# A gated state-space mix on one core: v's loads last and integer angles in the head, a room of its own for the ninth pair, three row products later, one group of output matmuls a scan later

## The chip, the core and the metric

The kernel runs on one core of one Trainium2 chip. Its time is the device time of one execution in microseconds; the measure is the median of several runs. One core has these engines, each with its own instruction stream: TensorE (PE) for matrix products, VectorE (DVE), ScalarE (ACT, which also evaluates functions from tables), GpSimd (POOL) and SyncE (SP). In this kernel SP starts nearly all loads and stores, and POOL starts the accumulating transfers: a transfer that adds what it reads to what stands in its target, called a gather below.

## What is computed

Two sequence layers over the same x (2048 steps, 1024 channels, bf16), mixed by a gate for each step:

```python
g = sigmoid((x * gate_w).sum(-1, keepdims=True))

# layer A: diagonal complex state space with 1024 states
Lam_bar = exp(dt * Lam)
Bu = einsum("bld,pd->blp", x, ((Lam_bar - 1) / Lam)[:, None] * Bmat)
for t in range(L):
    h = Lam_bar * h + Bu[:, t]
y_a = 2 * einsum("blp,dp->bld", hseq, Cmat).real + x * Dskip

# layer B: shift convolution of k (4 taps), times v, long convolution with ssm_k
kv = k_shift * v
y_b = x * (irfft(rfft(kv, 2S) * rfft(ssm_k, 2S))[:S] + kv * ssm_D)

out = g * y_a + (1 - g) * y_b
```

## The kernel before, in words

**Order.** Nothing is left to a scheduler on the four compute engines and SP. Every instruction goes through `put` (lines 92 to 95), which chains it behind the last one of the same engine; so every row of the profile has line 94, and groups are told apart by tiles. What the Python code calls first runs first on its engine. Most stages are generators: `step(x)` issues the next part of stage x, `steps(x, n)` the next n, `run(x)` the rest. `gather` (126) starts an accumulating transfer from POOL, `move` and `load_t` (a transposing load) start one from SP. Pools of tiles decide the rest: an instruction that writes a tile waits until the readers of the tile that had the room before are done. The pool `wu`, reached by `u4` (83), has three buffers of about 4 KB a partition, and `ps2` (86) hands out PSUM in four pieces of two banks.

**Layer B** goes over 8 tiles of 128 channels. `taps` (571) multiplies shifted columns of kT, the transposed k, by diagonal matrices `dg` on PE, and `times_v` multiplies by v on DVE. `fold_columns` or `fold_K` split the long filter into even and odd parts ("eok"), and `times_v` the same for the signal with its mirror image. `fwd_K` (634) and `fwd_V` (672) are forward transforms as matmuls with cosine and sine tables CF, SF and NCF (= -CF), in four steps `fi`; ACT evicts each result to KH (in BT[2], BT[3]) or Vh. `products` (685) multiplies the spectra on DVE, with gathers for some of the sums. `inverse` (767) transforms back with the tables CI and SI; ACT evicts to `cv`, and the result goes to a DRAM scratch, to be read back later by rows.

**The head** is channel tile 0, written out by hand (lines 157 to 174). Its loads on SP: two halves of kT, kn (the filter); v's first half is on ACT's queue, ahead of everything there but the small parameters, and v's second half on SP behind kn. DVE makes the angles of CF and SF in float32: the angle index over 4096 (`hf`), rounding with a large constant, the difference `rq` (`reduced`, 281), a Sin on ACT for SF, the absolute value on DVE, a Sin for CF. `first_times_v` (586) multiplies the tap sums by v straight from PSUM, forms the mirror image and its sum and difference. `first_K` (650) does the first two steps of the filter's transform, and evicts one on ACT and one on DVE. `inverse_angles` and `inverse_table` (382 to 398) make SI and CI from integer angles: an AND with 2047, an Abs on ACT (`fa`) and two Sin. `state_params` (418, "sp") computes from A's parameters the decay, the angles and the coefficients of all 8 tiles of states, in tiles of 128 x 8 or 16; its first part is an Exp on ACT (`dtv`), another table set than Sin. `taps(1)` starts the second channel tile, and its product with v on DVE (`ks<-ks,v`) is the start of a chain of DVE work.

**Layer A** goes over 4 blocks of 512 steps (tb) and 4 pairs of state tiles (g), 16 pairs in all. `Bu(i)` (833) multiplies x with B on PE for pair i of the list `order` (816), and ACT evicts to a tile U (odd and even steps apart). `turn_U` (922) scales the odd half by lambda on ACT to tiles Q and lets two gathers add it to the even half. U 6, 7, 8 and 15 come from the shared pool `wu`. `scan(tb, g)` (941) does the recurrence on DVE: turning by tables, four scan instructions, turning back; then it scales the states by lambda (`scaled`), on DVE, or for scans 4, 12, 13 and 14 on ACT into Q tiles, in which case the call is kept in `put_off` and made later. `sums` adds them to U's odd half during the next scan. `turn_C` turns the columns of C in the same way.

**Output rows.** 16 rows of 128 steps. For row k: `loads` reads layer B's result (pbb) and x (xr); `scale_b` (1076) scales pbb and Dskip's row on ACT, and a gather adds the two; `product` (1107) multiplies by x on DVE; `Cy_g` (1087) multiplies the states with C on PE; `scale_a` (1101) evicts from PSUM on ACT with the gate; `combine` (1111) starts a gather that adds the two; `store` writes the row out.

**The plan** (1433 to 1534) sets what stands between the scans. After scan j (`advance`), `plan[j]` names the PE work: "B9" is pair 9 of `Bu`, "C0" a whole output row, and "G23" is pair g = 3 of block 2 for all four rows of the block (`Cy_group`, 1471). With g = 3 the rows are done: for each of the four, `scale_a` and `combine` follow, and ahead of the first in block 2 the scaling that `put_off` holds. `multiplied[j]` names the row products that stand inside scan j, `scaled_b[j]` the rows whose `scale_b` comes after it; for a "G" entry they come ahead of the group. If `put_off` still holds a scaling when the plan entry is done, it is issued there. After the last scan the rows of block 3 follow: lines 1549 to 1567.

Of the kernel before, what the change touches and what calls it, by code (L numbers as in the profile page):

```python
# [15 lines left out]
MAGIC = 12582912.0  # L16
# [4 lines left out]
def kernel(  # L21
# [143 lines left out]
    for i, ap in enumerate((A_log_dt, A_Lambda_re, A_Lambda_im)):  # L165
        nc.scalar.dma_start(out=prow[i * ND:(i + 1) * ND, :], in_=ap.rearrange("(j p) -> j p", p=128))
    nc.scalar.dma_start(out=v0_half(0)[0], in_=v0_half(0)[1])
    pih = consts.tile([128, 1], F32, name="pih")
    put("dve", nc.vector.memset, pih, math.pi / 2.0)
    magic = consts.tile([128, 1], F32, name="magic")  # L170
    put("dve", nc.vector.memset, magic, MAGIC)

# [62 lines left out]
    for h in range(2):  # L235
        hs = slice(h * S // 2, (h + 1) * S // 2)
        load_t(kT0[:, PAD + hs.start:PAD + hs.stop], kf[hs, 0:128])
    load("kn", 0)
    move(*v0_half(1))
    lds["kT", 0], lds["v", 0] = kT0, v0  # L240
# [39 lines left out]

    def reduced(h, n):
        rq = u4([128, n], F32, "rq")
        ts(rq, h, MAGIC, -MAGIC, ALU.add, ALU.add)
        tt(rq, h, rq, ALU.subtract)
        return rq

    CF = tab_pool.tile([128, 2, 512], BF16, name="CF")
# [14 lines left out]


    stamp = consts.tile([128, 2], BF16, name="stamp")
    refl = consts.tile([128, 2, 128], BF16, name="refl")
# [8 lines left out]
    colm = consts.tile([128, 2], F32, name="colm")  # L314
    ts(colm, colm_i, 1.0 / 4096.0, None, ALU.mult)
    fr_ = u4([128, 512], F32, "fr_")
    copy(fr_, fr_i)
    pcol = consts.tile([128, 3 + KS, ND], F32, name="pcol")
# [5 lines left out]
    for k in range(KS):  # L324
        mm(psp[:, 1, k * ND:(k + 1) * ND], skr[:, :, k], ident[32:32 + ND, 32:32 + ND], True, True)
    hf = u4([128, 2, 512], F32, "h")
    for mt in range(2):
        ts(hf[:, mt], fr_, colm[:, mt:mt + 1], None, ALU.mult)
    copy(pcol[:, 3:], psp[:, 1, 0:KS * ND].rearrange("p (i j) -> p i j", j=ND))
# [37 lines left out]

    rqf = reduced(flat(hf), 1024)

    inv = {}  # L370

    def inverse_cols():
        colf = iota_i32([128, 2], [[512, 2]], 1, 4, "colf")
        inv["col"] = consts.tile([128, 2], F32, name="colneg")
        inv["at0"] = consts.tile([128, 2], F32, name="colat0")
        act(inv["col"], colf, func=ACT.Copy, scale=-1.0)
        act(inv["at0"], colf, func=ACT.Copy, scale=511.0)
        inv["less"] = consts.tile([128, 3], F32, name="less")
        for k, v in enumerate((-1024.0, -math.pi, -math.pi / 2.0)):
            nc.gpsimd.memset(inv["less"][:, k:k + 1], v)  # L380

# [8 lines left out]
    def inverse_table():  # L390

        hi, less, unit = flat(inv["room"]), inv["less"], TWO_PI / 2048.0
        fa = u4([128, 1024], F32, "fa")
        act(fa, hi, func=ACT.Abs, bias=less[:, 0:1])
        yield
        act(flat(SI), hi, func=ACT.Sin, scale=unit, bias=less[:, 1:2])
        yield
        act(flat(CI), fa, func=ACT.Sin, scale=unit, bias=less[:, 2:3])

# [18 lines left out]
    def state_params():  # L418

        dtv = small("dtv")  # L420
        act(dtv, logdt, func=ACT.Exp)
        yield
        abv = pair("abv")
        tt(abv, bc(dtv[:, None], [128, 2, NP]), pcol[:, 1:3], ALU.mult)
        yield
        act(rv, abv[:, 0], func=ACT.Exp)
        ts(thn, abv[:, 1], 1.0 / TWO_PI, None, ALU.mult)
        ts(nthn, abv[:, 1], -1.0 / TWO_PI, None, ALU.mult)
        yield
        th = pair("th")  # L430
        copy(th[:, 0], thn)
        ts(th[:, 1], thn, float(TB), None, ALU.mult)
        sq = pair("sq")
        tt(sq, pcol[:, 1:3], pcol[:, 1:3], ALU.mult)
        fr = pair("fr")
        ts(fr, th, MAGIC, -MAGIC, ALU.add, ALU.add)
        invden = small("invden")
        tt(invden, sq[:, 0], sq[:, 1], ALU.add)
        tt(fr, th, fr, ALU.subtract)
        put("dve", V.reciprocal, invden, invden)  # L440
        yield
# [208 lines left out]
    def first_K():  # L650

        eo, KH[0] = eos["k", 0], spectrum("K", 0)
        pss = [ps2([128, 2, 4, 128], "psk") for fi in range(2)]
        for mt in range(2):
            for fi, ps in enumerate(pss):
                fsl = slice(fi * 128, (fi + 1) * 128)
                for cc in range(2):
                    mm(ps[:, cc], (CF, SF)[cc][:, mt, fsl], eo[:, cc, mt], mt == 0, False)
                    mm(ps[:, cc, 1:4], (SF, NCF)[cc][:, mt, fsl], eo[:, 1 - cc, mt, 0:3], False, mt == 1)
                if mt == 1 and fi == 0:  # L660
                    act(of_tile(KH[0], fi), ps, func=ACT.Copy)
                elif mt == 1:
                    copy(of_tile(KH[0], fi), ps)

# [20 lines left out]
    def products(c, h=0, home=u4, by_dma=True):  # L685
# [147 lines left out]
    def Bu(i):  # L833
# [307 lines left out]
    step(columns)  # L1141
    sp = state_params()
    step(sp)
    step(first)
    ts(NCF, CF, -1.0, None, ALU.mult)
# [207 lines left out]
    load_CT(3)  # L1353
    with tc.tile_pool(name="fin", bufs=1, side="right") as fin:

        count = iter(range(16))

        def room(shape, dt, name):
            return fin.tile(shape, dt, name=name, tag=f"fin{next(count)}")

        prod, back = products(c, 0, room, False), inverse(c - 1)
        run(old)
        steps(prod, 3)
        run(turns_U[3])
        run(next(tiles))
        steps(turning[0], 2)
        step(back)
        run(back)
        gate(1)
        gate(2)  # L1370
        steps(prod, 2)
        b6, b7 = Bu(6)
        run(b6)
        run(b7)
        run(turns_U[6])
        run(turning[0])
        run(prod)
        load_xT(3)
        b8, b9 = Bu(7)
        run(b8)  # L1380
        run(b9)
        run(turning[1])
        b10, b11 = Bu(8)
        run(b10)
        run(b11)
    back = inverse(c)
# [37 lines left out]
    def Cy(tb, tl):  # L1424
        ps = ps2([128, 2, 512], "psy")
        for g in range(NG):
# [59 lines left out]
    for j in range(NS):  # L1486
# [109 lines left out]
```

## Time and profile before

| what | value |
|---|---|
| median of 3 runs | 379.9 us |
| the three runs | 379.87, 379.90, 380.58 us |
| time of the profiled execution | 381.04 us |
| its span, first to last instruction | 379.3 us |
| granted TensorE clock, mean | 1.00 |
| idle of ACT in the span | 71.7 us (379.3 - 307.6) |
| data moved by DMA | 71.78 MB, 189 GB/s |

Of the page's chain of work that ended last, this line tells whose work it was by engine:

```profile
DVE 55%; PE 26%; issue 8%; DMA 5%; ACT 4%; POOL 0%; SPq 0%; POOLq 0%; DVEq 0%
```

How to read the rows: a busy row of the page gives for each engine the busy time, its share of the span, and the number of instructions. A timeline row begins with the start in us from the span's beginning and the duration, then engine, line, operation, output <- inputs with their shapes, and how many equal instructions in a row it stands for (their first start, their whole length). What stands in brackets is the time for which the engine was idle just before, and what released it. PE is the matmul itself, PEld its weight load beside it. An engine that is idle in a row with no one waiting for it costs nothing.

### The profile page before, as it was taken

To read this page: it belongs to the slowest core of one execution; us is meant where nothing else is said; L and a number is where in the kernel's file an instruction comes from. 1 tells how busy PE (TensorE), PEld (TensorE's weight loads), DVE (VectorE), ACT (ScalarE), POOL (GpSimd) and SP (SyncE) were. 2 spreads that over 40 slices of the span, in tenths; PEclk is the share of its full clock that TensorE was granted. 3 is DMA by queue.
4 is the path that set the end of the run, shared out by engine and by line. 5 is a ranking of instruction groups with operands and counts; after the bars stand their busy time and mean duration, and the time that the engine had idled before them with its cause. 6 is when DMAs were issued, how large, how long until landed. Compare 5 with 4: busy or idle time off the path is not lost.

```text
span 379.3 us, 6647 instructions
## 1 busy us (share of the span) xinstructions
PE 369.9 (98%) x2434; PEld 200.3 (53%) x2469; DVE 364.1 (96%) x585; ACT 307.6 (81%) x473; POOL 79.1 (21%) x109
## 2 busy tenths in 40 slices
PE   7999999999999999999999999989999999999996
PEld 4656467575674847644544444434445444444444
DVE  8899999999999999999999999999999989969984
ACT  5879998988979899697949799998879868938501
POOL 4011030110301102021002012123443313635000
PEclk9999999999999999999999999999999999999999
DMA  7889999999999989968999999947998999998902
GB/s 168 168 114 264 215 213 189 236 218 203 228 200 185 215 166 194 179 145 153 207 183 209 215 186 253 256 101 131 197 247 138 251 247 204 160 255 146 221 0 111
DMA packets 126259, 71.78 MB, mean 189 GB/s; under 512 B 104649, under 2 KB 107601, under 8 KB 126226
## 3 DMA queue, kind: packets, MB, share of 16 engines
q1 hardware_dynamic: 112416, 45.90, 56.1%
q0 software_dynamic: 12688, 25.17, 38.7%
q10 hardware_dynamic: 1122, 0.28, 0.4%
q8 instruction: 19, 0.31, 0.3%
q14 instruction: 14, 0.11, 0.1%
HBM read 15.48 MB, written 8.39 MB: 63 GB/s over the span
## 4 chain that ended last, share of the span: by engine, by line
DVE 55%; PE 26%; issue 8%; DMA 5%; ACT 4%; POOL 0%; SPq 0%; POOLq 0%; DVEq 0%
PE psy L94 23%; DVE acc L94 20%; DVE wkh L94 13%; DVE A L94 5%; DVE Vh L94 4%; DVE t L94 3%; DVE U L94 2%; DVE ks L94 2%; DMA U<-Q 2%; ACT Q L94 2%; DVE trn L94 2%; PE taps L94 1%; DMA kT<-in_B_k_dram 1%; DMA BT<-gd 1%; DVE CT L94 1%
## 5 line engine op out<-in xcount | busy, mean ns | idle before, releaser
L94 PE MATMUL psy<-CT,U 128*128 128x512 bf16 (+1 forms) x418 | 92.7, 374 | 0.4
L94 PEld LDWEIGHTS <-U 128*128 128x128 bf16 x492 | 48.0, 98 | 57.3 <-issue 2.1
L94 PEld LDWEIGHTS <-BT 128*128 128x128 bf16 x544 | 50.5, 98 | 33.5 <-issue 0.2
L94 DVE TENSOR_TENSOR wkh<-BT,Vh 128x2048 bf16<-128x2048 bf16 (+3 forms) x31 | 44.6, 1457 | 0.0
L94 ACT ACTIVATE Q<-U,lam 128x512 bf16<-128x512 bf16 (+1 forms) x64 | 37.5, 632 | 8.5 <-DVE U L94 8.5
L94 POOL DMA_DIRECT2D U<-Q x26 | 26.6, 1033 | 82.9 <-ACT Q L94 42.4
L94 DVE TENSOR_TENSOR acc<-BT,Vh 128x4096 bf16<-128x4096 bf16 (+3 forms) x19 | 36.9, 1947 | 0.3 <-ACT Vh L94 0.2
L94 PE MATMUL both<-xT,BT 128*128 128x512 bf16 x157 | 35.2, 379 | 0.2
L94 ACT ACTIVATE Vh<-psv 128x1024 bf16<-128x1024 f32 x32 | 30.7, 1034 | 5.7 <-PE psv L94 5.6
L94 DVE TENSOR_TENSOR_SCAN A<-rv,init,A 128x256 bf16<-128x256 f32 x48 | 34.4, 738 | 0.0
L94 DVE TENSOR_TENSOR acc<-acc,wkh 128x1024 bf16<-128x1024 bf16 (+4 forms) x30 | 32.7, 1128 | 0.1
L94 ACT ACTIVATE U<-both 128x512 bf16<-128x512 f32 x44 | 24.2, 594 | 10.4 <-PE both L94 10.1
L94 ACT ACTIVATE BT<-psk 128x1024 bf16<-128x1024 f32 x31 | 30.0, 1035 | 2.3 <-PE psk L94 2.2
L94 POOL DMA_DIRECT2D acc<-wkh x8 | 9.7, 1218 | 100.7 <-DVE wkh L94 100.7
L94 PE MATMUL psk<-eok,SF 128*128 128x384 bf16 (+1 forms) x118 | 28.0, 354 | 0.2
L94 PEld LDWEIGHTS <-SF 128*128 128x128 bf16 x184 | 18.0, 98 | 19.1 <-issue 0.4
L94 PE MATMUL psz<-Vh,CI 128*128 128x512 bf16 x64 | 24.3, 379 | 0.0
L94 PE MATMUL psz<-Vh,SI 128*128 128x512 bf16 x64 | 24.3, 379 | 0.0
L94 PE MATMUL taps<-dg,kT 128*128 128x128 bf16 (+1 forms) x352 | 21.5, 208 | 1.0 <-DMA kT<-in_B_k_dram 1.0
L94 PEld LDWEIGHTS <-kT 128*128 128x128 bf16 x352 | 20.8, 99 | 2.5 <-DMA kT<-in_B_k_dram 2.0
L94 DVE TENSOR_TENSOR U<-U,trn 128x512 bf16<-128x512 bf16 (+1 forms) x58 | 21.2, 391 | 0.1
L94 PE MATMUL both<-xT,BTl 128*128 128x512 bf16 x94 | 21.1, 379 | 0.1
(223 smaller groups left out, 767.5 us busy)
## 6 DMA issues: line engine op xcount, KB each, us to landing
U<-Q POOLq DMA_DIRECT2D x26, 256.0 KB, 5.4
acc<-wkh POOLq DMA_DIRECT2D x6, 768.0 KB, 8.7
cv_scr<-cv SPq DMA_DIRECT2D x16, 256.0 KB, 4.8
kn<-in_B_ssm_k_dram SPq DMA_DIRECT2D x5, 512.0 KB, 3.7
v<-in_B_v_dram SPq DMA_DIRECT2D x5, 512.0 KB, 5.9
out_dram<-m SPq DMA_DIRECT2D x8, 256.0 KB, 4.8
BT<-cv_scr SPq DMA_DIRECT2D x7, 256.0 KB, 7.0
out_dram<-BT SPq DMA_DIRECT2D x7, 256.0 KB, 2.0
```

Of the source, the lines that this page charges most:

```text
L94: i = f(*a, **kw)
```

## The change

There are four parts.

- *Head.* v's first half leaves ACT's queue and goes on SP's, behind both halves of kT and kn. The angles of CF and SF become integers (minus the step times the odd index, then an AND with 4095), so `reduced` goes; the absolute value is an Abs on ACT to a tile `away`, and the Sin take scale and offset from `less`. The order is new: the first ACT part of `inverse_angles` comes right after CF and the second behind the folds, the parts of `state_params` later, NCF ahead of the products with v, `first_K` between the second of these and the mirror image. The second eviction of `first_K` goes from DVE to ACT. In `products(0, 0)` the first three pieces are in another order. Some parameter operations are placed in other parts of `state_params`.
- *A room.* The pool `fin`, which held one tile of channel tile 7's `products` for a limited stretch, stays open (in the diff only the lines that change more than their indentation), its tiles share one buffer, and U 8 (the ninth pair) is taken from it in place of `wu`.
- *Products.* Products 4, 7 and 11 leave scans 8, 10 and 12, and are issued after `advance` of these.
- *Group.* G23 moves from plan entry 12 to entry 13, ahead of which `scale_b` of row 15 stands; and so the put-off scaling of scan 12, which was issued inside G23, is issued at the end of entry 12, and the one issued inside G23 is that of scan 13.

```diff
@@ -166,7 +166,4 @@
         nc.scalar.dma_start(out=prow[i * ND:(i + 1) * ND, :], in_=ap.rearrange("(j p) -> j p", p=128))
-    nc.scalar.dma_start(out=v0_half(0)[0], in_=v0_half(0)[1])
     pih = consts.tile([128, 1], F32, name="pih")
     put("dve", nc.vector.memset, pih, math.pi / 2.0)
-    magic = consts.tile([128, 1], F32, name="magic")
-    put("dve", nc.vector.memset, magic, MAGIC)
 
@@ -238,2 +235,3 @@
     load("kn", 0)
+    move(*v0_half(0))
     move(*v0_half(1))
@@ -280,8 +278,2 @@
 
-    def reduced(h, n):
-        rq = u4([128, n], F32, "rq")
-        ts(rq, h, MAGIC, -MAGIC, ALU.add, ALU.add)
-        tt(rq, h, rq, ALU.subtract)
-        return rq
-
     CF = tab_pool.tile([128, 2, 512], BF16, name="CF")
@@ -303,2 +295,5 @@
 
+    less = consts.tile([128, 4], F32, name="less")
+    for k, v in enumerate((-2048.0, -1024.0, -math.pi, -math.pi / 2.0)):
+        nc.gpsimd.memset(less[:, k:k + 1], v)
     stamp = consts.tile([128, 2], BF16, name="stamp")
@@ -314,5 +309,3 @@
     colm = consts.tile([128, 2], F32, name="colm")
-    ts(colm, colm_i, 1.0 / 4096.0, None, ALU.mult)
-    fr_ = u4([128, 512], F32, "fr_")
-    copy(fr_, fr_i)
+    ts(colm, colm_i, -1.0, None, ALU.mult)
     pcol = consts.tile([128, 3 + KS, ND], F32, name="pcol")
@@ -325,5 +318,5 @@
         mm(psp[:, 1, k * ND:(k + 1) * ND], skr[:, :, k], ident[32:32 + ND, 32:32 + ND], True, True)
-    hf = u4([128, 2, 512], F32, "h")
+    hf = u4([128, 2, 512], I32, "h")
     for mt in range(2):
-        ts(hf[:, mt], fr_, colm[:, mt:mt + 1], None, ALU.mult)
+        ts(hf[:, mt], fr_i, colm[:, mt:mt + 1], None, ALU.mult)
     copy(pcol[:, 3:], psp[:, 1, 0:KS * ND].rearrange("p (i j) -> p i j", j=ND))
@@ -367,3 +360,3 @@
 
-    rqf = reduced(flat(hf), 1024)
+    ts(flat(hf), flat(hf), 4095, None, ALU.bitwise_and)
 
@@ -377,5 +370,2 @@
         act(inv["at0"], colf, func=ACT.Copy, scale=511.0)
-        inv["less"] = consts.tile([128, 3], F32, name="less")
-        for k, v in enumerate((-1024.0, -math.pi, -math.pi / 2.0)):
-            nc.gpsimd.memset(inv["less"][:, k:k + 1], v)
 
@@ -391,9 +381,9 @@
 
-        hi, less, unit = flat(inv["room"]), inv["less"], TWO_PI / 2048.0
+        hi, unit = flat(inv["room"]), TWO_PI / 2048.0
         fa = u4([128, 1024], F32, "fa")
-        act(fa, hi, func=ACT.Abs, bias=less[:, 0:1])
+        act(fa, hi, func=ACT.Abs, bias=less[:, 1:2])
         yield
-        act(flat(SI), hi, func=ACT.Sin, scale=unit, bias=less[:, 1:2])
+        act(flat(SI), hi, func=ACT.Sin, scale=unit, bias=less[:, 2:3])
         yield
-        act(flat(CI), fa, func=ACT.Sin, scale=unit, bias=less[:, 2:3])
+        act(flat(CI), fa, func=ACT.Sin, scale=unit, bias=less[:, 3:4])
 
@@ -419,2 +409,8 @@
 
+        sq = pair("sq")
+        tt(sq, pcol[:, 1:3], pcol[:, 1:3], ALU.mult)
+        invden = small("invden")
+        tt(invden, sq[:, 0], sq[:, 1], ALU.add)
+        put("dve", V.reciprocal, invden, invden)
+        yield
         dtv = small("dtv")
@@ -424,18 +420,11 @@
         tt(abv, bc(dtv[:, None], [128, 2, NP]), pcol[:, 1:3], ALU.mult)
-        yield
         act(rv, abv[:, 0], func=ACT.Exp)
-        ts(thn, abv[:, 1], 1.0 / TWO_PI, None, ALU.mult)
-        ts(nthn, abv[:, 1], -1.0 / TWO_PI, None, ALU.mult)
         yield
-        th = pair("th")
-        copy(th[:, 0], thn)
-        ts(th[:, 1], thn, float(TB), None, ALU.mult)
-        sq = pair("sq")
-        tt(sq, pcol[:, 1:3], pcol[:, 1:3], ALU.mult)
-        fr = pair("fr")
+        th, fr = pair("th"), pair("fr")
+        ts(th[:, 0], abv[:, 1], 1.0 / TWO_PI, None, ALU.mult)
+        ts(th[:, 1], abv[:, 1], TB / TWO_PI, None, ALU.mult)
+        copy(thn, th[:, 0])
         ts(fr, th, MAGIC, -MAGIC, ALU.add, ALU.add)
-        invden = small("invden")
-        tt(invden, sq[:, 0], sq[:, 1], ALU.add)
+        ts(nthn, thn, -1.0, None, ALU.mult)
         tt(fr, th, fr, ALU.subtract)
-        put("dve", V.reciprocal, invden, invden)
         yield
@@ -659,6 +648,6 @@
                     mm(ps[:, cc, 1:4], (SF, NCF)[cc][:, mt, fsl], eo[:, 1 - cc, mt, 0:3], False, mt == 1)
-                if mt == 1 and fi == 0:
+                if mt == 1:
                     act(of_tile(KH[0], fi), ps, func=ACT.Copy)
-                elif mt == 1:
-                    copy(of_tile(KH[0], fi), ps)
+                elif fi == 0:
+                    yield
 
@@ -702,6 +691,8 @@
 
-        def first(k):
+        split = c == 0 and h == 0
+
+        def first(k, fs=(0, 1)):
 
-            for f in range(2 if c == 0 and h == 0 else 1):
-                x = slice(f * 128, f * 128 + 128) if c == 0 and h == 0 else slice(0, w)
+            for f in fs if split else (0,):
+                x = slice(f * 128, f * 128 + 128) if split else slice(0, w)
                 tt(A[:, k, :, :, x], bc(K[:, k:k + 1, 0:1, x], [128, 2, 4, x.stop - x.start]), Vt[:, :, :, x], ALU.mult)
@@ -712,3 +703,8 @@
         if by_dma:
-            first(0)
+            if split:
+                first(0, (0,))
+                first(1, (0,))
+                first(0, (1,))
+            else:
+                first(0)
             yield
@@ -717,3 +713,3 @@
             yield
-            first(1)
+            first(1, (1,))
             yield
@@ -846,3 +842,5 @@
             shape = [128, 2 * (4 * HB + 4)]
-            if i in (6, 7, 8, 15):
+            if i == 8:
+                U = s5p["last"](shape, BF16, "U")
+            elif i in (6, 7, 15):
                 U = u4(shape, BF16, "U")
@@ -1130,2 +1128,3 @@
     step(first)
+    unit = TWO_PI / 4096.0
     trow[0] = tab_pool.tile([128, TB], mybir.dt.float16, name="row")
@@ -1133,9 +1132,10 @@
     inverse_cols()
-    act(flat(SF), rqf, func=ACT.Sin, scale=TWO_PI)
-    put("dve", V.scalar_tensor_tensor, out=flat(hf), in0=rqf, scalar=-1.0, in1=rqf, op0=ALU.mult, op1=ALU.max)
-    act(flat(CF), flat(hf), func=ACT.Sin, bias=pih, scale=-TWO_PI)
+    act(flat(SF), flat(hf), func=ACT.Sin, scale=unit, bias=less[:, 2:3])
+    away = u4([128, 1024], F32, "away")
+    act(away, flat(hf), func=ACT.Abs, bias=less[:, 0:1])
+    act(flat(CF), away, func=ACT.Sin, scale=unit, bias=less[:, 3:4])
+    angles = inverse_angles()
+    turns = inverse_table()
+    step(angles)
     columns = columns()
-    step(first)
-    fk = fold_columns(0)
-    step(fk)
     step(columns)
@@ -1143,12 +1143,13 @@
     step(sp)
-    step(first)
+    fk = fold_columns(0)
+    step(fk)
     ts(NCF, CF, -1.0, None, ALU.mult)
-    step(sp)
+    step(first)
+    step(first)
     run(fk)
-    angles = inverse_angles()
-    turns = inverse_table()
     step(angles)
-    step(angles)
-    step(sp)
+    fK = first_K()
+    step(fK)
     run(first)
+    run(fK)
     dg1 = dgs(1, True)
@@ -1157,5 +1158,5 @@
     load("kn", 1)
-    first_K()
     run(angles)
     fwd_V(0, (0, 1))
+    step(sp)
     step(turns)
@@ -1164,3 +1165,5 @@
     p0 = products(0, 0)
-    steps(p0, 3)
+    step(p0)
+    step(sp)
+    steps(p0, 2)
     run(columns)
@@ -1353,34 +1356,34 @@
     load_CT(3)
-    with tc.tile_pool(name="fin", bufs=1, side="right") as fin:
+    fin = pool("fin", 1, side="right")
 
-        count = iter(range(16))
+    def room(shape, dt, name):
+        return fin.tile(shape, dt, name=name, tag="fin")
 
-        def room(shape, dt, name):
-            return fin.tile(shape, dt, name=name, tag=f"fin{next(count)}")
+    s5p["last"] = room
 
...
@@ -1433,7 +1436,8 @@
     NS = NTB * NG
-    plan = ["", "B9 B10", "B11", "B12 B13 C0", "C1", "C2", "C3 B14", "B15", "G10", "G11", "G12 G13", "G20", "G21 G22 G23",
-            "", "", ""]
+    plan = ["", "B9 B10", "B11", "B12 B13 C0", "C1", "C2", "C3 B14", "B15", "G10", "G11", "G12 G13", "G20", "G21 G22",
+            "G23", "", ""]
     turned = dict(zip(range(3, 12), (8, 9, 4, 10, 11, 12, 13, 14, 15)))
     turned[0] = 7
-    multiplied = {4: (1,), 5: (2,), 6: (3,), 8: (4,), 9: (5,), 10: (6, 7), 11: (8,), 12: (9, 10)}
+    multiplied = {4: (1,), 5: (2,), 6: (3,), 9: (5,), 10: (6,), 11: (8,), 12: (9, 10)}
+    behind = {8: 4, 10: 7, 12: 11}
     loaded = {7: (7, 8), 8: (9, 10), 9: (11, 12), 10: (13,), 11: (14,), 12: (15,)}
@@ -1449,4 +1453,2 @@
             run(turning[6])
-        if j == 12:
-            product(11)
 
@@ -1493,2 +1495,4 @@
         advance(j)
+        if j in behind:
+            product(behind[j])
         for t in turning[2 * j:2 * j + 2]:
```

More of the change, by code (lines that the diff above doesn't have):

```diff
@@ L424, in state_params @@
         tt(abv, bc(dtv[:, None], [128, 2, NP]), pcol[:, 1:3], ALU.mult)
+        act(rv, abv[:, 0], func=ACT.Exp)
         yield
-        act(rv, abv[:, 0], func=ACT.Exp)
-        ts(thn, abv[:, 1], 1.0 / TWO_PI, None, ALU.mult)
-        ts(nthn, abv[:, 1], -1.0 / TWO_PI, None, ALU.mult)
-        yield
-        th = pair("th")
-        copy(th[:, 0], thn)
-        ts(th[:, 1], thn, float(TB), None, ALU.mult)
-        sq = pair("sq")
-        tt(sq, pcol[:, 1:3], pcol[:, 1:3], ALU.mult)
-        fr = pair("fr")
+        th, fr = pair("th"), pair("fr")
+        ts(th[:, 0], abv[:, 1], 1.0 / TWO_PI, None, ALU.mult)
+        ts(th[:, 1], abv[:, 1], TB / TWO_PI, None, ALU.mult)
+        copy(thn, th[:, 0])
         ts(fr, th, MAGIC, -MAGIC, ALU.add, ALU.add)
-        invden = small("invden")
-        tt(invden, sq[:, 0], sq[:, 1], ALU.add)
+        ts(nthn, thn, -1.0, None, ALU.mult)
         tt(fr, th, fr, ALU.subtract)
-        put("dve", V.reciprocal, invden, invden)
         yield
@@ L1143 @@
     step(sp)
+    fk = fold_columns(0)
+    step(fk)
+    ts(NCF, CF, -1.0, None, ALU.mult)
     step(first)
-    ts(NCF, CF, -1.0, None, ALU.mult)
-    step(sp)
+    step(first)
     run(fk)
-    angles = inverse_angles()
-    turns = inverse_table()
     step(angles)
-    step(angles)
-    step(sp)
+    fK = first_K()
+    step(fK)
     run(first)
+    run(fK)
     dg1 = dgs(1, True)
@@ L1353 @@
     load_CT(3)
-    with tc.tile_pool(name="fin", bufs=1, side="right") as fin:
-        count = iter(range(16))
-        def room(shape, dt, name):
-            return fin.tile(shape, dt, name=name, tag=f"fin{next(count)}")
[L1361 to L1385, printed above, removed]
+    fin = pool("fin", 1, side="right")
+    def room(shape, dt, name):
+        return fin.tile(shape, dt, name=name, tag="fin")
+    s5p["last"] = room
+    prod, back = products(c, 0, room, False), inverse(c - 1)
+    run(old)
+    steps(prod, 3)
+    run(turns_U[3])
+    run(next(tiles))
+    steps(turning[0], 2)
+    step(back)
+    run(back)
+    gate(1)
+    gate(2)
+    steps(prod, 2)
+    b6, b7 = Bu(6)
+    run(b6)
+    run(b7)
+    run(turns_U[6])
+    run(turning[0])
+    run(prod)
+    load_xT(3)
+    b8, b9 = Bu(7)
+    run(b8)
+    run(b9)
+    run(turning[1])
+    b10, b11 = Bu(8)
+    run(b10)
+    run(b11)
     back = inverse(c)
```

## The prediction

> **What bounds the kernel now.** I read the page's busy times first, then the windows, the chain in order of time, and the timelines of the three places that the change touches. From the page and from the windows (columns: stretch, its length, busy time and count of PE, PEld, DVE, ACT, POOL, granted clock, DMA share, GB/s):
>
> ```profile
> PE 369.9 (98%) x2434; PEld 200.3 (53%) x2469; DVE 364.1 (96%) x585; ACT 307.6 (81%) x473; POOL 79.1 (21%) x109
> ```
>
> ```profile
> 230.00:240.00 10.00, 9.95 (x47) 4.51 (x46) 10.00 (x23) 9.90 (x16) 3.73 (x5) 1.00 1.20 236
> 240.00:250.00 10.00, 8.76 (x40) 3.92 (x40) 9.90 (x25) 9.94 (x15) 1.83 (x3) 1.00 0.94 217
> 340.00:360.00 20.00, 19.95 (x93) 9.10 (x93) 20.00 (x42) 13.87 (x18) 6.10 (x7) 1.00 0.92 188
> ```
>
> A full stretch holds 47 matmuls of 512 columns in 10 us, 0.21 us each, at a granted clock of 1.00. PE is packed; the stretch from 240 has 40. So time is won only where PE stands still, and lost wherever PE comes to stand. The chain (start, length, engine):
>
> ```profile
> 22.02 1.09 DVE ks L94
> ...
> 43.48 1.22 DVE Vh L94
> ```
>
> PE has two stalls of note of its own, 0.97 us in the head at 7.48 and 1.51 us at 250.32 (rows below; in brackets stands the idle time before a row and what ended it). In between the chain runs through DVE, which from 22 us has no wait worth naming until 289; PE takes Vh at 43.6 as soon as DVE has half of it. So what the head does to DVE at 22 us is what it is worth.
>
> **Part 1, the head** (v's loads, integer angles, the new order).
>
> ```profile
> 4.34 2.17 PE L94 MATMUL taps<-dg,kT 128*128 128x128 bf16 x32
> 4.16 1.10 DVE L94 TENSOR_SCALAR rq<-h 128x1024 f32<-128x1024 f32 x1
> 5.29 1.23 DVE L94 TENSOR_TENSOR rq<-h,rq 128x1024 f32<-128x1024 f32 x1
> 6.55 1.06 ACT L94 ACTIVATE SF<-rq 128x1024 bf16<-128x1024 f32 x1 [0.65 <-DVE rq L94]
> 7.48 1.96 PE L94 MATMUL taps<-dg,kT 128*128 128x128 bf16 x32 [0.97 <-DMA kT<-in_B_k_dram]
> 7.81 1.15 ACT L94 ACTIVATE CF<-h,pih 128x1024 bf16<-128x1024 f32 x1 [0.20 <-DVE h L94]
> 8.98 1.28 ACT L94 ACT_TABLE_LOAD   x1
> 9.81 1.23 DVE L94 TENSOR_TENSOR ks<-taps,v 128x1024 bf16<-128x1024 f32 x1
> 10.27 0.21 ACT L94 ACTIVATE dtv<-pcol 128x8 f32<-128x8 f32 x1
> 10.95 0.42 DVE L94 TENSOR_SCALAR NCF<-CF 128x1024 bf16<-128x1024 bf16 x1
> 14.46 1.02 ACT L94 ACTIVATE BT<-psk 128x1024 bf16<-128x1024 f32 x1 [0.17 <-PE psk L94]
> 15.24 1.22 DVE L94 CAST BT<-psk 128x1024 bf16<-128x1024 f32 x1
> 16.09 1.94 ACT L94 ACTIVATE Vh<-psv 128x1024 bf16<-128x1024 f32 x2 [0.60 <-PE psv L94]
> 16.37 0.68 DVE L94 TENSOR_SCALAR BT<-BT 128x1024 int32<-128x1024 int32 x1
> 17.91 1.16 ACT L94 ACTIVATE fa<-BT,less 128x1024 f32<-128x1024 int32 x1
> 20.52 1.02 ACT L94 ACTIVATE ks<-taps 128x1024 bf16<-128x1024 f32 x1 [0.55 <-PE taps L94]
> 21.94 1.18 DVE L94 TENSOR_TENSOR ks<-ks,v 128x2048 bf16<-128x2048 bf16 x1
> ```
>
> With v's first half behind kT and kn on SP's queue, kT's second half can land before the first taps end (4.34 + 2.17 = 6.51): PE gains up to 0.97; 0 if the transposes are slow by themselves. I take 0.9. DVE drops rq (1.10), rq (1.23), its negation and a cast, and hands a copy of psk (1.22) to ACT, for one integer AND (0.68): some 4.5 us less work. Little of that reaches PE, for two waits.
>
> First, v comes last, and NCF now stands ahead of v's products on DVE. It waits for CF: SF starts near 5.3 (the AND ends at 5.0, the row's iota comes two selects sooner), then `away` (1.16, as fa) and CF (1.15) end it at 8.65. NCF 0.42, then two products 1.14 apart end at 11.4, against 9.81 + 1.23 = 11.04. The mirror and both sums are no earlier than before; the K matmuls put between them only fill PE, whose psv ends 0.7 sooner.
>
> Second, ACT. From its first K copy at about 13.75 (0.7 sooner, with PE) it does two K copies (2.0), two Vh (1.95), the Exp table load, which stood behind CF and now stands here (1.28), dtv (0.2), fa (1.05 to the next) and two tap copies (1.95): 22.2, against 20.52 + 1.02 = 21.54. DVE's `ks<-ks,v` needs the last one, so it starts at 22.15 instead of 21.94: **+0.2**. PE's 0.7 ends at Vh. Bounds: -0.6 (ACT hidden, PE's lead kept) to +0.6 (v lands later than NCF). The small parameter operations moved stay ten; they lie in DVE's waits for dtv, and without that cover would cost 10 x 0.09 us.
>
> By the Trainium skill ("ScalarE: Activation LUTs", What ACT_TABLE_LOAD costs) a switch of table sets costs a 1.28 us load and a drain of 1.38 us more; by it the head would be +1.6. This trace shows the load alone: dtv starts at 10.27, 1.29 after it.
>
> **Part 2, the ninth pair's room.**
>
> ```profile
> 212.57 0.22 ACT L94 ACTIVATE U<-ends 128x4 bf16<-128x4 bf16 x1 [2.51 <-DMA U<-Q]
> 213.90 0.38 PE L94 MATMUL psz<-Vh,SI 128*128 128x512 bf16 x1
> 215.02 1.93 ACT L94 ACTIVATE cv<-psz 128x1024 bf16<-128x1024 f32 x2
> 249.19 2.06 ACT L94 ACTIVATE U<-both 128x512 bf16<-128x512 f32 x4
> 250.32 1.02 PE L94 MATMUL psy<-CTa,U 128*128 128x512 bf16 x4 [1.51 <-ACT U L94]
> ```
>
> U 8 shared three buffers, and ACT stood 2.51 us for a gather to leave one. In its own room it waits for DVE's products of some 10 us before. ACT's lead is cut by PE: the second cv needs the psz that ends at 213.90 + 0.38 = 214.28; it began at 215.02 + 0.97 = 215.99, so 1.6 is kept. ACT has no idle from there to 250 (9.90 and 9.94 of 10 busy), so the lead arrives: the second of the four evictions at 249.19, which frees the bank for psy, ends at 248.65 instead of 250.25, before PE asks (250.32 - 1.51 = 248.81). PE gains 1.5 (bounds 0 and 1.5); with the head, PE, ACT and the gathers that follow them run **1.3 early** from 250.
>
> **Part 3, products and the group** (rows of DVE, ACT, PE, POOL; then two narrow DMA windows, whose last number is us from issue to landing).
>
> ```profile
> 289.58 0.69 DVE L94 TENSOR_TENSOR BT<-BT 128x1024 bf16<-128x1024 bf16 x1 [0.74 <-issue]
> 310.22 0.69 DVE L94 TENSOR_TENSOR xr<-xr,pbb 128x1024 bf16<-128x1024 bf16 x1 [1.31 <-DMA pbb<-gd]
> 337.52 0.69 DVE L94 TENSOR_TENSOR row<-row 128x1024 bf16<-128x1024 bf16 x1 [3.07 <-issue]
> 343.84 2.09 ACT L94 ACTIVATE BT<-psy,gcols 128x1024 bf16<-128x1024 f32 x2
> 349.18 2.54 ACT L94 ACTIVATE Q<-V,lam 128x512 bf16<-128x512 bf16 x4
> 347.97 1.03 PE L94 MATMUL psy<-CTa,U 128*128 128x512 bf16 x4
> 337.39 1.33 POOL L94 DMA_DIRECT2D U<-Q  x1
> 344.87 0.86 POOL L94 DMA_DIRECT2D U<-Q  x1 [5.27 <-ACT Q L94]
> ```
>
> ```profile
> U<-Q POOLq DMA_DIRECT2D x1, 256.0 KB, 7.0
> ...
> U<-Q POOLq DMA_DIRECT2D x1, 256.0 KB, 3.4
> ```
>
> Products 4, 7 and 11 stand in front of scans and wait 0.74 + 1.31 + 3.07 = 5.1 us for their gathers; behind the scans they wait for nothing, and DVE runs up to 5 us ahead. PE does not wait for DVE there, so this is worth nothing by itself.
>
> The moved group costs. Today ACT evicts block 2's rows (scale_a of rows 8 to 11, from 343.84) before it scales scan 13 (`Q<-V`, 349.18). With G23 at scan 13, scale_b of row 15 and the four scalings come first, and the evictions queue behind. The last two scalings write the fourth Q buffer, which the last gather into U 15 must have read: issued at 344.87, landed 3.4 later, 348.27. Scan 13 itself is ready sooner (348.9 - 5.0 = 343.9). So ACT stands at 348.27 - 1.3 = 346.97, two scalings take 1.25, one eviction 1.05, the handovers 0.1: 349.4. The next block's first matmul needs that bank; it ran at 347.97 and now arrives at 346.7, to wait 2.7. **+1.4** for all that follows, which is packed to the end. On POOL row 15's gather passes the four combines, and those rows' stores come 5 us later, with 20 us left.
>
> Sum: head +0.2, gap -1.5, new wait +2.7 = +1.4. The profiled execution took 381.04 with a span of 379.3, 1.7 around it; the median is 379.9. So span 380.7, time 382.4 in its terms, **381.3** on the median.
>
> **The rivals.**
> - *The last gathers land early, and the wait is not there* (not slower). If both gathers into U 15 take the lone one's 3.4, the second is issued at 337.39 + 3.4 + 0.5 and landed at 344.7, less 1.3 is 343.4; the bank is free at 345.8, before 346.7. PE keeps 1.3: 378.6. Against: the first took 7.0 in a full queue. By the Trainium skill ("DMA: Bandwidth & Descriptors", Anatomy of one DMA) such a gather takes 2.0 + 0.6 us, an estimate from its fit, and this would hold; the rows disagree. 0.15.
> - *The gap at 250 stays* because ACT meets another wait on its way (a CT load). Then nothing is early: landing 348.3, bank 350.7, +2.7 + 0.2: 382.8. 0.1.
> - *The head costs more*: ACT's chain before `ks<-ks,v` slips by another 1.2 (a table load's worth): 382.5. 0.05.
> - *The head pays*: DVE at 22 us earlier by PE's 0.7 to 1.0 instead of later; all shifts, 380.2. 0.1.
>
> **How the numbers follow.** The forecast has 0.6, with a range of its own of 380.4 to 382.2. A measurement tells about 0.2% (0.76 us), so the borders are 379.1 and 380.7. Slower: 0.55 of the forecast's 0.6, 0.1 and 0.05, 0.7. Same: 0.05, most of the head's 0.1, 0.03 of the first rival, 0.18. Faster 0.12. The range of 379.2 to 382.9 leaves out little more than the first rival.
>
> **What would show it.** Right: no ACT wait before U 8's ends; PE's stall at 250 gone; a PE wait of 2 to 3 us before the last block's first psy, ended by ACT's eviction; ahead of it ACT idle before the second pair of `Q<-V`, ended by `U<-Q`. DVE without its three waits. The head: taps without the 0.97, `ks<-ks,v` at 22.0 to 22.4. Wrong: that psy at 347 or before, `ks<-ks,v` under 21.5, or a gap left at 250.

## The result, and the profile after

| | before | after |
|---|---|---|
| median, 20 runs each | 379.88 us | 381.56 us |
| lowest run | 378.72 us | 380.62 us |
| the profiled execution, its span | 381.04, 379.3 us | 380.70, 378.9 us |

The ratio of after to before is 1.0043 with a 95% interval of 1.0028 to 1.0058: slower by 1.6 us (1.1 to 2.2). The forecast was 381.3. Mind the last row: the two profiled executions say the opposite, -0.4 us. The profiled execution of before lies 1.16 us above its kernel's median, that of after lies among the fastest of its kernel. So a difference between these two traces is not yet a difference between the kernels, and most of the experiments below serve to tell the two apart. (The medians are over all runs, while the ratios and their intervals leave out disturbed executions; the profiled executions of the group alone and of the first kernel with the early Exp were disturbed too, from about 210 and 240 us on, and are not read behind that point.)

From the timelines of the changed kernel, at the places that the prediction priced:

```profile
4.44 2.20 PE L94 MATMUL taps<-dg,kT 128*128 128x128 bf16 x32 [0.17 <-DMA kT<-in_B_k_dram]
6.68 1.96 PE L94 MATMUL taps<-dg,kT 128*128 128x128 bf16 x32
9.61 2.36 DVE L94 TENSOR_TENSOR ks<-taps,v 128x1024 bf16<-128x1024 f32 x2 [0.34 <-DMA v<-in_B_v_dram]
17.95 1.28 ACT L94 ACT_TABLE_LOAD   x1
19.24 0.21 ACT L94 ACTIVATE dtv<-pcol 128x8 f32<-128x8 f32 x1
20.40 1.92 ACT L94 ACTIVATE ks<-taps 128x1024 bf16<-128x1024 f32 x2
22.35 1.23 DVE L94 TENSOR_TENSOR ks<-ks,v 128x2048 bf16<-128x2048 bf16 x1
44.06 0.39 PE L94 MATMUL psz<-Vh,CI 128*128 128x512 bf16 x1 [0.62 <-DVE Vh L94]
...
248.83 1.02 PE L94 MATMUL psy<-CTa,U 128*128 128x512 bf16 x4
...
331.31 0.86 POOL L94 DMA_DIRECT2D U<-Q  x1 [5.87 <-ACT BT L94]
332.60 1.33 POOL L94 DMA_DIRECT2D U<-Q  x1
337.76 1.33 ACT L94 ACTIVATE Q<-U,lam 128x512 bf16<-128x512 bf16 x2 [0.60 <-DMA U<-Q]
341.23 0.86 POOL L94 DMA_DIRECT2D U<-Q  x1 [6.42 <-ACT BT L94]
344.03 2.56 ACT L94 ACTIVATE Q<-V,lam 128x512 bf16<-128x512 bf16 x4 [2.85 <-DVE V L94]
346.49 4.10 ACT L94 ACTIVATE BT<-psy,gcols 128x1024 bf16<-128x1024 f32 x4
347.64 1.02 PE L94 MATMUL psy<-CTa,U 128*128 128x512 bf16 x4 [1.00 <-ACT BT L94]
```

The head is much as drawn: the second taps follow the first without the 0.97 us, `ks<-ks,v` starts at 22.35 (predicted 22.0 to 22.4), and what PE had won it gives back at 44.06, where it now waits 0.62 us for DVE. One step differs: the products with v wait 0.34 us for v itself, where the prediction had them wait for NCF. The stall at 250 is gone; PE comes to `psy` at 248.83. And before the last block's first `psy` PE waits for ACT's eviction, as forecast, but 1.0 us and not 2.7, and the four scalings ahead of it waited for DVE (2.85 us, `Q<-V`), not for a gather. Two of the three terms of the sum are therefore in doubt: is the stall at 250, worth 1.5 us in the one trace of before, there in every execution, and what sets the new wait?

### The profile page after: what moved, and what is told of

It is laid out like the page before. It is cut to its first block, busy times and chain, and to the rows that moved or that the text cites. A ratio compares the mean times of both kernels' runs of the same rounds, so it can differ in the third digit from the quotient of the medians.

```text
span 378.9 us, 6645 instructions
## 1 busy us (share of the span) xinstructions
PE 370.3 (98%) x2434; PEld 200.0 (53%) x2469; DVE 360.3 (95%) x580; ACT 309.5 (82%) x475; POOL 79.2 (21%) x110
## 4 chain that ended last, share of the span: by engine, by line
DVE 78%; PE 10%; issue 8%; ACT 3%; DMA 1%; DVEq 0%; ACTq 0%
DVE acc L94 20%; DVE A L94 15%; DVE wkh L94 13%; DVE U L94 9%; PE psy L94 7%; DVE trn L94 6%; DVE Vh L94 4%; DVE t L94 3%; DVE ks L94 3%; DVE CT L94 1%; DVE BT L94 1%; PE taps L94 1%; DVE ev L94 1%; DVE xr L94 1%; DMA kT<-in_B_k_dram 1%
## 5 line engine op out<-in xcount | busy, mean ns | idle before, releaser
L94 ACT ACTIVATE BT<-psk 128x1024 bf16<-128x1024 f32 x32 | 31.0, 1036 | 2.7 <-PE psk L94 2.6
L94 PE MATMUL psk<-eok,SF 128*128 128x512 bf16 (+1 forms) x117 | 27.8, 354 | 0.2
```

Of the source, the lines that this page charges most:

```text
L94: i = f(*a, **kw)
```

## The experiments

In each, "theory 1" is the prediction's account, "theory 2" the one formed from the two traces: the stall at 250 belongs to the profiled execution alone, and the new wait is that of scan 13's states on DVE. Ratios and their intervals are against the kernel before on the same chip.

**The parts one at a time.** The head alone (the whole diff up to `steps(p0, 2)`, nothing of `Bu`, `fin` and the plan):

> The head's edits alone, the rest as before. Both theories: slower by little, +0.2 by the prediction (bounds -0.6 to +0.6), +0.4 by the profile of the changed kernel, whose ks<-ks,v starts at 22.35 instead of 21.94: 380.1 to 380.3. Theory 1 (the prediction): PE's stall at 250 is in every execution, so this profile shows about 1.5 us of it. Theory 2 (rival, formed from the two profiles, whose spans differ by -0.4 while the medians differ by +1.7): the stall at 250 was in the one profiled execution of before and is missing in most; this profile then shows less than 0.5 us there.

Measured: 380.25 us, ratio 0.9992 (0.9968 to 1.0017). U 8's room alone (and the pool `fin` kept open, as in the change):

```diff
-            if i in (6, 7, 8, 15):
+            if i == 8:
+                U = s5p["last"](shape, BF16, "U")
+            elif i in (6, 7, 15):
```

> U 8's own room alone, the rest as before. Theory 1: PE wins the 1.5 us of the stall at 250 and nothing takes them back, 378.4. Theory 2: most executions have no such stall, so nothing is won, 379.9 within 0.4.

Measured: 379.61 us, ratio 0.9978 (0.9950 to 1.0006). The three products alone (out of `multiplied` and `between`):

```diff
+    behind = {8: 4, 10: 7, 12: 11}
...
         advance(j)
+        if j in behind:
+            product(behind[j])
```

> Products 4, 7 and 11 behind their scans, all else as before. Prediction: worth nothing by itself, 379.9 within 0.4, though DVE loses its waits of 0.7, 1.3 and 3.1 us and scan 13's states are ready 5 us sooner. Rival: DVE's place counts for the tail, -0.5 or more.

Measured: 380.39 us, ratio 1.0003 (0.9986 to 1.0021). Products and group together (the diff from `plan` on), head and room as before:

> Products 4, 7 and 11 and the group G23 later, head and room as before. Theory 1: the last two scalings of scan 13 wait for the gather into U 15 (348.27), the bank comes free at 350.7 where PE came at 347.97: +2.7, 382.6. Theory 2: the gather is not what ACT waits for; scan 13's states are ready at 344.0 as in the profile of the changed kernel, four scalings and one eviction end at 347.6, and PE, without the stall at 250, comes at 346.5: +1.2, 381.1.

Measured: 383.54 us, ratio 1.0053 (1.0015 to 1.0090). So only the part with the group in it is slower clear of its interval; head, room and products are each within 0.25% of nothing.

The room's interval still holds theory 1's 378.4 us (0.9960), so the times of this kernel alone don't decide; the profiles do. All of these kernels have U 8 in the shared pool as before: the first row of each pair is ACT's first instruction on U 8 with its wait for the gather, the second PE's `psy` at about 250. Head alone, whose PE has no row with an idle time there:

```profile
211.14 0.22 ACT L94 ACTIVATE U<-ends 128x4 bf16<-128x4 bf16 x1 [0.88 <-DMA U<-Q]
```

Products alone:

```profile
213.00 0.22 ACT L94 ACTIVATE U<-ends 128x4 bf16<-128x4 bf16 x1 [1.73 <-DMA U<-Q]
250.75 1.02 PE L94 MATMUL psy<-CTa,U 128*128 128x512 bf16 x4 [0.73 <-ACT U L94]
```

And the kernel before, once more, as it stands:

> The kernel before once more, as a second profile of it and as a measure of the comparison itself: ratio 1.000 within 0.002. Theory 1 of the stall at 250 (there in every execution): 1.5 us again. Theory 2 (a rare landing of the gather that ACT waits for at 212): ACT waits 0.8 to 0.9 us there and PE has less than 0.5 us at 250.

```profile
210.63 0.22 ACT L94 ACTIVATE U<-ends 128x4 bf16<-128x4 bf16 x1 [1.22 <-DMA U<-Q]
248.39 1.02 PE L94 MATMUL psy<-CTa,U 128*128 128x512 bf16 x4 [0.23 <-ACT U L94]
...
331.52 0.86 POOL L94 DMA_DIRECT2D U<-Q  x1 [5.97 <-issue]
332.81 1.33 POOL L94 DMA_DIRECT2D U<-Q  x1
341.68 0.86 POOL L94 DMA_DIRECT2D U<-Q  x1 [6.66 <-issue]
346.04 1.03 PE L94 MATMUL psy<-CTa,U 128*128 128x512 bf16 x4
```

It measured 380.56 us, ratio 1.0024 (0.9999 to 1.0050): a kernel against itself, so a ratio of 0.25% in a comparison of this size is no finding. Together with the 2.51 and 1.51 us of the first trace the rows make one line: ACT's wait for the gather is 2.51, 1.73, 1.22, 0.88, and PE's stall 40 us later is that wait less 1.0 us: 1.51, 0.73, 0.23, none. ACT has 1.0 us to spare; what comes beyond it reaches PE whole. What differs is the time that the gathers take: ACT goes on 12.6, 11.8, 11.3 and 11.0 us after POOL issued the first of the two in front of it (at 199.95, 201.16, 199.30 and 200.14). Two more profiles with U 8 in the shared pool fit the line, with waits of 0.81 us (products and group, below) and none (the head with the early Exp, below), and no PE stall. So three of these six have a stall at 250, 0.4 us on the average of the six, and the profiled execution of before had the longest. In the room's own profile and in that of the changed kernel neither wait is there, but in most executions there is little to win. Theory 2 was too narrow: the stall isn't rare, it has a size of its own in each execution.

The three POOL rows of this second trace of before answer the other question too. They are the last gathers into U 14 and U 15. In the first trace they were issued at 336.09, 337.39 and 344.87, here at 331.52, 332.81 and 341.68, and nothing in the code differs. The gather that lands at 348.27, on which the prediction built its new wait, was later by 3.2 us in that one execution. Not all of this counts: PE, too, is 1.9 us later there (347.97 against 346.04 at the last block's first `psy`), so against PE the gather was late by 1.3 us.

**What sets the new wait.** The group alone, products left inside their scans:

```diff
-    ... "G20", "G21 G22 G23", "", "", ""]
+    ... "G20", "G21 G22", "G23", "", ""]
```

> G23 at plan entry 13 alone, products, head and room as before. Theory 2 (what ACT waits for is scan 13's states on DVE): with the three products still in front of the scans, DVE has them at 348.9 as before; four scalings (2.5) and one eviction (1.05) end at 352.4, and PE comes at 346.5 to 348.0: a stall of 4.5 to 6 us, 384.4 to 385.9. Theory 1 (ACT waits for the gather into U 15 at 348.3): the products change nothing, +2.7 as in the prediction, 382.6.

Measured: 386.48 us, ratio 1.0179 (1.0153 to 1.0204), 6.8 us slower. The products are worth 4.8 us here (1.0179 less 1.0053, on two chips; the changed kernel on the chip of this run, below, is 5.1 us faster). Theory 2 says why: with them in front DVE has scan 13's states 5 us later, and ACT, which has the scalings ahead of the evictions, is held that long. This is argued from the order, as the profile of this kernel is not read there. Nor does the run speak against the prediction itself: it took the later of two times, and without the products moved its own 348.9 for scan 13 would have been the later. That the products change nothing was theory 1's wording here, not the prediction's; what ends ACT's wait is told by the profiles below. Still the products, worth nothing alone, are what makes the moved group bearable. The run is 0.8 us slower than the stall of 6 us that theory 2 allowed at most; that remainder stays open.

Then ACT's order alone: G23 stays at entry 13, but the put-off scalings of scan 13 go behind the four evictions.

```diff
             if g == NG - 1:
-                if tb == 2 and tl == 0:
-                    put_off.pop()()
                 scale_a(k, [(slice(0, D), flat(ps))])
```

> The changed kernel with G23 at entry 13, but the scalings of scan 13 issued behind the four evictions. If the cost of the moved group is ACT's order alone, PE has no stall before the last block's first psy, and the time is that of the kernel with G23 back at 12, 379.9 to 380.5; DVE then waits some 3 us for the scalings of scan 13, and nobody for DVE. Rival: the gathers or DVE's place also matter, the time stays at 381.4 or above.

Measured: 380.24 us, ratio 1.0010 (0.9985 to 1.0035). From its timelines:

```profile
338.86 1.33 ACT L94 ACTIVATE Q<-U,lam 128x512 bf16<-128x512 bf16 x2 [1.69 <-DMA U<-Q]
342.17 2.17 ACT L94 ACTIVATE BT<-psy,gcols 128x1024 bf16<-128x1024 f32 x2
344.96 1.11 ACT L94 ACTIVATE BT<-psy,gcols 128x1024 bf16<-128x1024 f32 x1 [0.61 <-PE psy L94]
346.69 1.11 ACT L94 ACTIVATE BT<-psy,gcols 128x1024 bf16<-128x1024 f32 x1 [0.61 <-PE psy L94]
347.70 2.54 ACT L94 ACTIVATE Q<-V,lam 128x512 bf16<-128x512 bf16 x4
```

The evictions now keep up with PE (before the last two ACT waits 0.61 us for it), PE has no idle time before the last block, and DVE waits in its place, 2.4 us for the scaled states of scan 13, and no later PE wait comes of it. The changed kernel itself, once more on the same chip:

> The changed kernel once more, for a second profile of it and for a comparison on the same chip: ratio 1.0043, 381.5. Theory 2: PE's stall before the last block's first psy is 1.2 to 2.5 us, ACT's wait ahead of the scalings of scan 13 is ended by DVE, not by a gather. Theory 1: a stall of 2.7 us, ended by the landing of the last gather into U 15.

Measured: 381.34 us, ratio 1.0040 (1.0018 to 1.0062), and in its profile:

```profile
338.68 1.33 ACT L94 ACTIVATE Q<-U,lam 128x512 bf16<-128x512 bf16 x2 [1.48 <-DMA U<-Q]
344.62 2.56 ACT L94 ACTIVATE Q<-V,lam 128x512 bf16<-128x512 bf16 x4 [2.52 <-DVE V L94]
348.22 1.02 PE L94 MATMUL psy<-CTa,U 128*128 128x512 bf16 x4 [1.15 <-ACT BT L94]
```

Between these two kernels only ACT's order differs, and the medians differ by 1.1 us, the size of PE's stall (1.0 and 1.15 us in the two profiles of the changed kernel). The intervals of the two ratios overlap, so the times alone would not show it; the profiles, with the stall and without it, do. In the profile of products and group the same stall is larger, and its rows show how a gather does come in, one scan earlier than the prediction had it:

```profile
339.25 1.33 ACT L94 ACTIVATE Q<-U,lam 128x512 bf16<-128x512 bf16 x2 [2.40 <-DMA U<-Q]
340.61 0.43 DVE L94 TENSOR_TENSOR U<-U,Q 128x512 bf16<-128x512 bf16 x1 [1.36 <-ACT Q L94]
345.17 2.56 ACT L94 ACTIVATE Q<-V,lam 128x512 bf16<-128x512 bf16 x4 [2.52 <-DVE V L94]
347.64 4.10 ACT L94 ACTIVATE BT<-psy,gcols 128x1024 bf16<-128x1024 f32 x4
348.79 1.86 PE L94 MATMUL psy<-CTa,U 128*128 128x512 bf16 x4 [2.33 <-ACT BT L94]
```

ACT's second pair of scalings of scan 12 (`Q<-U`) waits 2.40 us for the gather that reads its buffer; DVE needs this pair for the sums inside scan 13 and waits 1.36 us; so scan 13's states, ACT's next scalings and the evictions are all later by that. In the two profiles of the changed kernel ACT's wait is 0.60 and 1.48 us, DVE's none and 0.44, and PE's stall 1.00 and 1.15, against 2.40, 1.36 and 2.33 here.

Last, G23 back at entry 12 and all else as changed:

> The changed kernel with G23 back at plan entry 12 (head, room and products as changed). Theory 1: the new wait of 2.7 goes, PE keeps 1.3: 378.6. Theory 2: the wait of 1.2 goes and the head's +0.4 stays: 380.3. Both: no PE stall before the last block's first psy.

Measured: 380.43 us, ratio 1.0008 (0.9982 to 1.0035). Without the group the change is no change that could be measured; theory 1's 378.6 (0.9966) lies outside. In none of the eight profiles with G23 at entry 12 that are read there does PE wait before the last block's first `psy`.

**The head.** The prediction held ACT's chain of evictions, table load and `fa` to be what delays `ks<-ks,v`. ACT stands idle for 1.65 us just before the first psk eviction, so the Exp with its load can go there (G23 at entry 12):

```diff
     step(angles)
+    step(sp)
     fK = first_K()
...
     fwd_V(0, (0, 1))
-    step(sp)
     step(turns)
```

> The changed kernel with G23 back at 12, and the Exp with its table load put into ACT's idle time before the first psk eviction (ACT idle 1.65 us up to 14.16 in the changed kernel). If ACT's chain of evictions, table load and fa sets ks<-ks,v, as the prediction has it, that chain is 1.5 us shorter: ks<-ks,v at 21.3 to 21.7 instead of 22.1 to 22.35, PE's new stall at 44 shrinks from 0.6 to 1.4 us to under 0.3, and the time falls by 0.4 to 0.8 against the kernel with G23 back at 12: about 379.5. Rival: DVE's own work ahead of ks<-ks,v sets it, then nothing changes: 380.0 to 380.4.

Measured: 379.00 us, ratio 0.9984 (0.9968 to 1.0000). Its profile has `ks<-ks,v` at 21.71 and no PE stall at 44. That looked like a version that beats both. So once more, and the same head with nothing else changed:

> Head with the early Exp, room and products, G23 at 12, once more for an undisturbed profile: 379.0, no PE stall at 44, at 250 or before the last block's first psy. The room and the products are worth nothing beside the head if this is within 0.3 of the same head alone; the room is worth something in the executions in which its gather lands late if it is lower.

> The head's edits with the Exp and its table load in ACT's idle time, room, products and group as before. If PE's gain in the taps (0.97) is kept once ks<-ks,v is no later, PE has no stall at 44 and the time falls by 0.6 to 1.0: 379.0 to 379.3. If the room or the products are needed for it: 379.9.

Measured: 380.09 us, ratio 1.0004 (0.9980 to 1.0028), and 379.83 us, ratio 1.0004 (0.9985 to 1.0023), both on another chip. The gain didn't come again, and what made the first measurement lower stays open. The profiles show why the head of one execution can't be taken for another's. First the early Exp's first profile, then that of the same code again:

```profile
4.51 1.96 PE L94 MATMUL taps<-dg,kT 128*128 128x128 bf16 x32 [0.25 <-DMA kT<-in_B_k_dram]
6.52 1.96 PE L94 MATMUL taps<-dg,kT 128*128 128x128 bf16 x32
21.71 1.22 DVE L94 TENSOR_TENSOR ks<-ks,v 128x2048 bf16<-128x2048 bf16 x1
```

```profile
4.53 3.18 PE L94 MATMUL taps<-dg,kT 128*128 128x128 bf16 x32 [0.26 <-DMA kT<-in_B_k_dram]
7.75 1.96 PE L94 MATMUL taps<-dg,kT 128*128 128x128 bf16 x32
13.09 1.22 DVE L94 TENSOR_TENSOR BT<-ks,mirror 128x1024 bf16<-128x1024 bf16 x1 [1.07 <-PE mirror L94]
17.84 1.90 DVE L94 TENSOR_TENSOR acc<-BT,Vh 128x1024 bf16<-128x1024 bf16 x3 [1.02 <-ACT Vh L94]
22.47 1.22 DVE L94 TENSOR_TENSOR ks<-ks,v 128x2048 bf16<-128x2048 bf16 x1
```

The same 32 matmuls start at the same time and take 1.96 us in the one and 3.18 us in the other. With PE 1.2 us late, DVE waits longer for the mirror image and for Vh (1.07 and 1.02 us against 0.68 and 0.67), and `ks<-ks,v` is 0.76 us later. With PE on time the place of the Exp counts: 21.71 against 22.35 with the late Exp in the changed kernel, where v's products start at the same time (9.64 and 9.61). But ACT's last tap copy is not alone in it. The first row is of the changed kernel, the second of the first profile with the early Exp:

```profile
19.48 0.17 DVE L94 TENSOR_TENSOR abv<-dtv,pcol 128x16 f32<-128x16 f32 x1 [0.54 <-ACT dtv L94]
...
20.28 1.02 ACT L94 ACTIVATE ks<-taps 128x1024 bf16<-128x1024 f32 x1 [0.37 <-PE taps L94]
```

With the late Exp DVE, too, waits for it (0.54 us for dtv) and then has no wait up to 22.35, which is when ACT's copies end (20.40 + 1.92 = 22.32): two chains meet there. With the early Exp ACT's copies end at 21.30, 0.4 us before `ks<-ks,v`, and it is DVE's own work that sets it.

## Why the prediction came out right

The time was right (381.56 for 381.3) and so was the sign; the sum was not right term by term. Two terms were too large, by 0.7 and 1.6 us, and as they have opposite signs the errors cancelled in part. That the total came within 0.3 us is luck as much as it is the mechanism.

- *The head, +0.2: right within what could be measured.* The head alone measured 0.9992 (0.9968 to 1.0017), which agrees with +0.2 and with nothing. `ks<-ks,v` starts at 21.43 to 22.07 in the six profiles with the old head and at 22.04 to 22.35 in the five with the new one and the late Exp, 0.4 us later on the average. kT's second half came in time, and PE's lead goes back at 44 (0.62 us there), as the prediction said in taking DVE's delay for the head's worth. Two things it left out: v lands behind NCF (it had this in its upper bound only), and DVE's own chain behind its wait for dtv ends at the same moment as ACT's tap copies. PE's gain is one only when PE is at full rate.
- *The stall at 250, -1.5: mis-sized.* The mechanism was right: the wait goes with the room, the lead arrives, and PE came to `psy` at 248.83 without a wait, where 248.81 was its free time in the trace of before. The step that failed is "ACT stood 2.51 us for a gather" taken as a constant. In the other five profiles it stands 0 to 1.73 us, the first 1.0 of it costs nothing, the stall is 0.4 us on the average of all six, and the room's kernel was 0.8 us faster (-1.9 to +0.2) instead of 1.5.
- *The new wait, +2.7: right place, wrong releaser, mis-sized.* The step that failed is "the last two scalings write the fourth Q buffer, which the last gather into U 15 must have read", with 348.27 less 1.3 as its time. In the changed kernel that gather was issued at 341.23 and took 3.3 us to land, so at 344.5 it was out of the way of the third scaling, which had its turn at 345.3. What was left is a number that the prediction had and took for the earlier of the two: scan 13 ready at 343.9. From there 2.5 for four scalings and 1.05 for an eviction make 347.5, and PE, which asked at 346.6, went on at 347.64.
- *The first rival* (the gathers land early) happened, but not for its reason: the first gather into U 15 took 8.1 us, not 3.4, and was issued at 332.60 instead of 337.39. Its conclusion didn't come either: the wait is then shorter, not gone, because DVE's states come next.
- *Products and POOL:* the products are worth nothing alone, as said; "worth nothing by itself" hid that the moved group needs them, which the prediction used only as "scan 13 itself is ready sooner". Row 15's gather in front of the combines, and the late stores, showed no cost: with the evictions first, both are as in the changed kernel, and the ratio is 1.0010.

Two parts add up: all but the group +0.3 us (1.0008; -0.7 to +1.3), ACT's order +1.1 us, together 1.4 of the measured 1.6. Taken singly, head, room and products make -0.3, -0.8 and +0.1 us, where the three together made +0.3; the intervals, each of about 1 us either way, allow both, so the room's 0.8 is not shown to be there in the whole change.

The Trainium skill's figure for a change of table sets ("ScalarE: Activation LUTs", What ACT_TABLE_LOAD costs) includes a drain of 1.38 us. As in the trace of before, the trace shows none: in the changed kernel the load at 17.95 takes 1.28 us and the next activation follows at once.

## What to carry to other kernels

A landing time in a trace is one draw. Before a stall that ends at a DMA goes into a sum with its full length, take a second profile of the same code, and ask how much of the wait the engine can spare; here two draws of the same unlucky execution made two wrong terms. And where two chains lead to one instruction, the later one in a trace need not be the later one in the next. When work is moved behind other work on an in-order engine, price it from every input of what now stands in front, not only from the latest of one trace. And a move that is free alone may be the cover of another: test them together and apart.

## What was not expected of the hardware

PE's rate in the first microseconds is not the same in every execution, and the granted clock doesn't show it. In the windows view of the second profile with the early Exp (the same columns as in the prediction's windows) the clock reads 1.00 while 16 matmuls start in two microseconds and, later, 36:

```profile
4.00:6.00 2.00, 1.74 (x16) 1.48 (x16) 0.74 (x3) 1.32 (x5) 0.97 (x3) 1.00 1.04 171
...
8.00:10.00 2.00, 2.00 (x36) 1.95 (x34) 1.60 (x7) 1.61 (x2) 0.11 (x1) 1.00 0.80 147
```

Start to start, tap matmuls stand 0.107 us apart at first and 0.056 us from one moment on. In thirteen of the fourteen profiles that moment lay between 4.7 and 7.4 us into the span, at 4.8 in before and at 5.0 in after; in the first profile with the early Exp the taps had the fast rate from their start at 4.51. The kernel's own warm-up matmuls of 512 columns stand 0.40 to 0.43 us apart, the slow rate, against 0.21 later. The Trainium skill ("TensorE: Matmul & The Clock Gate", What's actually happening) describes a clock gate that opens after a busy window of 3.4 us in a free-running grid of such windows. With the first matmul at 1.19 that puts the moment, as an estimate by this page, between 4.6 and 8.0, which agrees but for the 0.1 us by which the 4.51 lies ahead of it; the half microsecond either way that the page gives for the spread doesn't agree.

For this change it matters in one way. In the head of before PE waits for kT's second half in any case, and a late change of rate hides in that wait. Products alone, with that head and the moment at 7.3:

```profile
4.57 5.01 PE L94 MATMUL taps<-dg,kT 128*128 128x128 bf16 x64 [0.22 <-DMA kT<-in_B_k_dram]
```

The taps end at 9.58, against 7.48 + 1.96 = 9.44 in the first trace of before, where the moment came early. With the wait gone they end at 6.52 + 1.96 = 8.48 or 7.75 + 1.96 = 9.71 in the two profiles above: the difference of 1.23 us comes from the moment at which the rate changes, and it is more than the 0.97 us that the earlier transfer had won.
